# Attention over channels followed by a mixture of adapters: a planner with a finer model of the DMA rings, and the order of work that comes out of it

## The chip, the cores and the metric

The kernel runs on one core of a Trainium2 chip. Its time is the device time of one execution in microseconds (us), lower is better. A core has a matrix engine (TensorE, PE in the profile), two engines for elementwise work (VectorE, DVE; ScalarE, ACT), GpSimd (POOL) and SyncE (SP), which here issue transfers, and 16 DMA engines that all transfers share. A chunk below is 128 rows of 256 numbers, one row per SBUF partition.

## The reference

Four batches of q, k and v, each 6400 x 256 in float32. Columns of q and k are normalized over the 6400 rows; a 256 x 256 score matrix per batch goes through a softmax and multiplies v. Of the result x (25600 x 256) eight small adapters of rank 16 are gated, the two best of each row kept.

```python
qn = q / (norm(q, axis=1) + 1e-06);  kn = k / (norm(k, axis=1) + 1e-06)
a = softmax(kn.transpose(0, 2, 1) @ qn / tau)        # [4, 256, 256]
x = (v @ a).reshape(25600, 256)
logits = x @ w_gate                                  # 8 experts
topk = the two largest of each row;  w = softmax over these two
out = x + sum over the two of w * ((x @ A[e]) @ B[e])
```

## The kernel before, in words

**Tiles.** A batch is 50 chunks. q and k of a batch come in three pieces each of 17, 17 and 16 chunks (`QK`); v comes in five pieces of 10 chunks (`V`), and so does the output. The loads read float32 and write bfloat16 into SBUF, which is why GpSimd issues them (line 578, one instruction for a piece). Only the first four chunks of q and of k of batch 0 come as float32, by SyncE and ScalarE (line 574), into an output slot, and ScalarE casts them. The output is stored in float32 by SyncE (line 928): one store of 1,280 KB per piece, and for the last two pieces three stores each (512, 512, 256 KB; `FINE`).

**Work of a batch.** For each chunk, `G` adds k-transposed times q to two PSUM accumulators (line 593) and, unless the chunk's group is in the set `OFF`, the squares of k (line 597) and q (602), for the norms. For a group in `OFF` (a group is five or six chunks of either q or k) ScalarE squares it instead (line 615, step `sq`) and VectorE adds the groups up (line 621, `add`). After chunk 49 a short chain of small steps on all engines (`accs`, `n2`, `rsqrt`, `rq_ps`, `s`, `exp`, `aT`, `waA`, `a`) turns the accumulators into the softmax matrix and its product with the gate and the first adapter weights (`waA`).

For each piece of v: `T` transposes it on TensorE (line 788), `Te` brings it to SBUF (`vT`), then the gate logits and the first adapter product: a piece in the set `MERGED` makes both in one product (`ZL`, line 812) and copies them to SBUF (`ZLe`, four copies); another piece makes the logits alone (`log`, line 826), and later the adapter product (`Z`, line 879). Eight small VectorE steps and a tanh on ScalarE form the gate; `Ze` multiplies (line 890); `gzT` transposes the gated values (line 902); `Y` computes attention output plus the second adapter product into PSUM, two chunks at a time, five for a piece (lines 915 and 920); `Ye` copies them to an output slot on ScalarE or VectorE (lines 769 and 771); `store` sends the slot off.

**Order.** Nothing is ordered by hand except the loads. `make_plan` writes down every step with the engine or engines it may run on, the time it takes, a rank, and the buffers it takes and gives back (`STORE`: six PSUM banks, six q or k pieces, three v pieces, four transposed pieces, seven output slots, and so on). `Plan.run` then plays the program through once in Python, before anything runs: an engine that is free takes the ready step with the lowest rank, a load is issued when its buffer is free and fewer than eight are out, and two queues of transfers, loads and stores, share a bandwidth. The order in which steps were started is the order in which each engine's instructions are written; the chip then keeps that order engine by engine and waits on semaphores for the data. So the planner's numbers do not delay anything on the chip by themselves, they only choose the order.

The constants that steer it: `WORDS` is the order of the loads after the three pieces of batch 0's q and k (`q10` is piece 0 of batch 1's q and k together, `v23` piece 3 of batch 2's v). `AHEAD` and `SQ` move the ranks of transposes and squares forward, `SAFE` is a reserve that the planner adds to a load's landing, `HEAD` the time before the first transfer moves. `HOLD` names stores that wait until a given load has landed, so that they do not take DMA time from loads before that. It is done by a tiny transfer on SyncE's queue (step `hold`, line 645): it copies 16 numbers of the last chunk of that load to a scrap tile, so it waits for the load, and every store behind it on SyncE's queue waits too. `FIRST` and `PARTS` split the first and last q and k pieces. Every output slot and every v slot is a tile of its own, taken from the pool under a name with its number.

Of the kernel before, what the change touches and what calls it, by code (L numbers as in the profile page):

```python
# [18 lines left out]
class Step:  # L19
# [3 lines left out]
    def __init__(self, key, eng, deps, rank, take, give, size=0.0):  # L23
        self.packet = max(size, 0.08)
        self.key, self.eng, self.deps, self.rank = key, eng, deps, rank
        self.take, self.give, self.size = take, give, size
        self.users, self.place = [], {}
        self.ready, self.end, self.on = 0.0, None, None
        self.left = len(deps)
        self.only = next(iter(eng)) if len(eng) == 1 else None  # L30
# [38 lines left out]
class Plan:  # L69

    LAT = 0.07
    DMA_LAT = 1.8
    ENGINES = ("PE", "DVE", "ACT", "POOL", "SP")
    ISSUE = 0.55
    ISSUE_LAT = 1.8
    STORE_LAT = 1.4
    OUT = 8

# [15 lines left out]

    def run(self, head):
# [4 lines left out]
        loads, queue, stores = list(self.loads), [], []  # L100
        now, out, left = 0.0, 0, sum(s.key[0] != "warm" for s in self.steps.values())
        free["POOL"] = 0.2
        clock = Clock()

# [5 lines left out]
        def can_take(s):  # L110
            return all((kind, name) in held or self.store[kind] for kind, name in s.take)

        def start(s, eng):
            for kind, name in s.take:
                if (kind, name) not in held:
                    held[kind, name] = self.store[kind].pop(0)
                    s.place[kind] = held[kind, name]
            s.on = eng
            s.t = now
            self.out.append(s)  # L120

# [5 lines left out]
        while left:  # L127
            again = False
            if (loads and free["POOL"] <= now + 1e-9 and out < self.OUT and can_take(loads[0])):
                s = loads.pop(0)  # L130
                start(s, "POOL")
                out += 1
                free["POOL"] = now + self.ISSUE
                push(free["POOL"], "free", None)
                push(now + self.ISSUE_LAT, "asked", s)
                again = True
            for e in self.ENGINES:
# [3 lines left out]
                for s in wait[e]:  # L141
                    if not can_take(s) or (s.key[0] == "warm" and not clock.idle(now)):
                        continue
# [3 lines left out]
                    if best is None or (s.rank, s.seq) < (best.rank, best.seq):  # L147
                        best = s
# [9 lines left out]
                else:  # L158
                    push(free[e], "end", best)
# [3 lines left out]
            busy = [x for x in (queue, stores) if x]  # L163
            t = events[0][0] if events else float("inf")
            base = max(now, head)

            share = sum(x[0].packet for x in busy)
            if busy:
                t = min(t, base + min(x[0].size / x[0].packet for x in busy) * share)
            assert t < float("inf"), [s.key for s in self.steps.values() if s.end is None][:20]  # L170
            if t > base:
                for x in busy:
                    x[0].size -= (t - base) * x[0].packet / share
                    if x[0].size < 1e-6:
                        push(t + self.DMA_LAT, "landed", x[0])
                        out -= x is queue
                        x.pop(0)
            now = max(now, t)
            while events and events[0][0] <= now + 1e-9:
                _, _, what, s = heapq.heappop(events)  # L180
                if what == "asked":
                    queue.append(s)
                elif what == "store":
                    stores.append(s)
# [3 lines left out]
                elif what == "landed":  # L188
                    push(now + (SAFE if s.on == "POOL" else 0.0), "end", s)
                    for u in s.users:  # L190
                        if u.key[0] == "hold":
                            u.left -= 1
                            if u.left == 0:
                                push(now, "ready", u)
                elif what == "end":
# [6 lines left out]
                    for u in s.users:  # L202
                        u.left -= u.key[0] != "hold"
                        if u.left == 0 and u.eng and u.key[0] != "hold":
                            push(now + (0.0 if s.on == u.only else self.LAT), "ready", u)
# [10 lines left out]
V = ((0, 1), (1, 1), (2, 1), (3, 1), (4, 1))  # L216
# [13 lines left out]

def make_plan(B, order, ahead):
# [6 lines left out]
    for kind, b, i in order:  # L238
        if kind == "v":
            p.add(("load", "v", b, i, V[i][0] * PC, V[i][1] * PC), {}, (), 0, take=(("v", (b, i)),),  # L240
                  size=LOAD * V[i][1] * PC + 0.062)
            continue
        for c, n in PARTS.get((b, i), QK[i:i + 1]):
            for h in "qk":
                p.add(("load", h, b, i, c, n), {}, (), 0, take=(("qk", (h, b, i)),), size=LOAD * n + 0.062)

    for h in "qk":
        p.add(("cast", h), {"ACT": 0.6}, [("load", h, 0, 0) + PARTS[0, 0][0]], 0)
    p.loads[2].size += 0.5
    for b in range(B):  # L250

        for i, (c0, n) in enumerate(QK):
            for c in range(c0, c0 + n):
# [8 lines left out]
                p.add(("G", b, c), {"PE": 0.442 - 0.112 * sum((b, group_of(c), w) in OFF for w in "kq")}, deps,  # L262
# [4 lines left out]
        for w in "kq":  # L267
# [5 lines left out]
            for x, g in enumerate(halves):  # L273
                c, n = GROUPS[g]
                i = max(i for i, q in enumerate(QK) if q[0] <= c)
                p.add(("sq", w, b, g), {"ACT": 0.2 + 0.2125 * n},
                      [k for k in p.steps if k[:4] == ("load", w, b, i) and k[4] < c + n and c < k[4] + k[5]]
                      + [("cast", w)] * ((b, c) == (0, 0)), pos["qk", b, i] - SQ, take=(("ssq", (w, b)) if x == 0 else ("sq", (w, b, g)),),
                      give=(("qk", (w, b, i)),))
                if x:  # L280
                    p.add(("add", w, b, g), {"DVE": 0.15 + 0.268 * n},
# [4 lines left out]
            if halves:  # L286
                p.add(("red", w, b), {"DVE": 1.9}, [before], pos["qk", b, len(QK) - 1] - 1, give=(("ssq", (w, b)),))
                p.add(("n2p", w, b), {"PE": 0.35}, [("red", w, b), ("G", b, NC - 3)], -100, take=(("bank", ("n2p", w, b)),))
# [698 lines left out]
```

## Time and profile before

| | before |
|---|---|
| median of 3 runs (254.35 to 254.46) | 254.4 us |
| profiled execution, its own time | 254.46 us |
| its span | 252.7 us |
| mean granted TensorE clock | 0.986 |
| busy: TensorE, VectorE, ScalarE, GpSimd | 217.8, 192.7, 151.1, 27.1 us |
| HBM read and written | 78.91 MB and 26.21 MB, 416 GB/s over the span |
| loads issued by GpSimd (20 of v, 14 each of q and k), KB written each | 640; 512 to 1,088 |
| stores of the output | 18 of 1,280 KB, 4 of 512 KB, 2 of 256 KB |

The page of a profile shows the span in 40 slices of 6.3 us; each digit is the busy share of a slice in tenths, and a row of GB/s says what the DMA engines moved. A casting load counts there with the bytes it writes, half of those it reads. A second part lists the DMA queues: q0 is the queue of GpSimd's loads, q1 that of SyncE's stores. A third follows the work that ended last back through what released it. A table of stretches gives the busy time of every engine between two instants (the number of instructions in brackets), then the granted clock, the DMA share and GB/s; the DMA share can exceed 1, because packets of two queues overlap in the records.

### The profile page before, as it was taken

What the parts mean: (1) busy time and instruction counts of PE and PEld (TensorE: products, weight loads), DVE (VectorE), ACT (ScalarE), POOL (GpSimd) and SP (SyncE); (2) the same over time, 40 slices, a digit from 0 to 9 for tenths busy, and PEclk for the clock granted to TensorE, in tenths of its full rate; (3) what the DMA queues carried; (4) which work ended last, traced back from release to release, by engine and by line L of the source; (5) the groups of instructions that cost most, each with busy time, mean ns of one, the idle gap of its engine ahead of it and who ended that gap; (6) DMA issues with size and microseconds to landing.
All of it is one profiled execution on the core that took longest, in us unless ns stands there. A gap on an engine that the chain in (4) does not pass through costs nothing.

```text
span 252.7 us, 5852 instructions
## 1 busy us (share of the span) xinstructions
PE 217.8 (86%) x2357; PEld 193.0 (76%) x2357; DVE 192.7 (76%) x528; ACT 151.1 (60%) x269; POOL 27.1 (11%) x54
## 2 busy tenths in 40 slices
PE   0274995988999998689999999889999979999990
PEld 0162882876999996579899899779999769999980
DVE  0055589869899987588899899489898898889850
ACT  5454427546786543975667768362674846657671
POOL 7003010040002002000500100500000000000000
PEclk9998899999999999999999999999999999999997
DMA  8999999999999999999999999999999999999996
GB/s 251 217 217 209 211 223 208 217 218 215 215 217 241 303 305 298 224 213 221 210 215 220 215 217 217 211 212 313 317 251 353 322 341 317 337 392 415 404 408 249
DMA packets 11243, 66.70 MB, mean 264 GB/s; under 512 B 1360, under 2 KB 1744, under 8 KB 6608
## 3 DMA queue, kind: packets, MB, share of 16 engines
q0 software_dynamic: 6912, 38.80, 74.4%
q1 hardware_dynamic: 3968, 26.87, 26.1%
q10 hardware_dynamic: 336, 0.66, 0.8%
q8 instruction: 18, 0.29, 0.4%
q14 instruction: 9, 0.07, 0.1%
HBM read 78.91 MB, written 26.21 MB: 416 GB/s over the span
## 4 chain that ended last, share of the span: by engine, by line
PE 53%; DMA 32%; issue 5%; DVE 4%; ACT 2%; POOL 1%; POOLq 0%; DVEq 0%
DMA v<-in_v_dram 18%; PE Y_ps L915 13%; PE acc L593 10%; DMA qk<-in_q_dram 10%; PE Y_ps L920 6%; PE T_ps L788 5%; PE ZL_ps L812 5%; DMA qk<-in_k_dram 5%; PE gzT_ps L902 4%; PE acc L597 3%; PE acc L602 2%; PE Z_ps L879 1%; ACT a_exp L715 1%; DVE a_bf L763 1%; PE log_ps L826 1%
## 5 line engine op out<-in xcount | busy, mean ns | idle before, releaser
L593 PE MATMUL acc<-qk 128*128 128x256 bf16 x400 | 69.6, 282 | 17.0 <-DMA qk<-in_k_dram 9.4
L915 PE MATMUL Y_ps<-a_bf,vT 128*128 128x256 bf16 x400 | 60.0, 273 | 0.2 <-DVE acc_sb L710 0.2
L621 DVE TENSOR_TENSOR ssq<-ssq,sq 128x1280 f32<-128x1280 f32 (+1 forms) x27 | 43.4, 1606 | 19.6 <-ACT sq L615 19.6
L769 ACT COPY y<-Y_ps 128x512 f32<-128x512 f32 x79 | 46.2, 586 | 16.6 <-PE Y_ps L920 13.5
L593 PEld LDWEIGHTS <-qk 128*128 128x128 bf16 x400 | 34.2, 101 | 20.7 <-DMA qk<-in_k_dram 11.5
L615 ACT ACTIVATE sq<-qk 128x1280 f32<-128x1280 bf16 (+1 forms) x27 | 36.9, 1368 | 17.7 <-DVE ssq L621 16.6
L915 PEld LDWEIGHTS <-vT 128*128 128x128 bf16 x400 | 38.9, 98 | 4.7 <-issue 0.3
L920 PE MATMUL Y_ps<-ball,gzT 128*128 128x256 bf16 x200 | 38.2, 273 | 0.0
L597 PE MATMUL acc<-qk 128*128 128x128 bf16 x242 | 34.5, 224 | 0.0
L788 PE MATMUL T_ps<-ident,v 128*128 128x128 f32 x200 | 27.6, 274 | 0.6 <-DVE waA_sb L757 0.4
L769 ACT COPY vT<-T_ps 128x512 f32<-128x512 f32 (+1 forms) x44 | 21.2, 510 | 10.9 <-PE T_ps L788 10.5
L597 PEld LDWEIGHTS <-qk 128*128 128x128 bf16 x242 | 24.4, 101 | 3.5
L890 DVE TENSOR_TENSOR gz<-zl,gateg 128x256 bf16<-128x256 f32 x70 | 26.3, 445 | 0.3
L578 POOL DMA_DIRECT2D v<-in_v_dram x20 | 11.5, 576 | 133.7 <-PE T_ps L788 92.8
L788 PEld LDWEIGHTS T_ps<-ident,v 128*128 128x128 f32 x200 | 22.3, 141 | 1.6 <-DVE waA_sb L757 0.6
L602 PE MATMUL acc<-qk 128*128 128x128 bf16 x168 | 23.4, 222 | 0.0
L902 PE MATMUL gzT_ps<-ident,gz 128*128 128x128 f32 x100 | 20.9, 281 | 2.6 <-DVE gateg L868 1.4
L920 PEld LDWEIGHTS <-gzT 128*128 128x128 bf16 x200 | 19.6, 98 | 2.3
L812 PE MATMUL ZL_ps<-waA_sb,vT 128*128 128x136 bf16 x280 | 19.5, 223 | 1.7 <-DVE waA_sb L757 1.5
L771 DVE COPY gzT<-gzT_ps 128x256 f32<-128x256 f32 (+1 forms) x40 | 15.0, 380 | 7.1 <-PE gzT_ps L902 5.6
L812 PEld LDWEIGHTS <-vT 128*128 128x128 bf16 x280 | 17.7, 98 | 2.4 <-issue 2.1
L615 ACT ACTIVATE ssq<-qk 128x1536 f32<-128x1536 bf16 x8 | 11.9, 1489 | 11.4 <-DMA qk<-in_q_dram 7.4
(80 smaller groups left out, 271.3 us busy)
## 6 DMA issues: line engine op xcount, KB each, us to landing
out_dram<-y SPq DMA_DIRECT2D x18, 1280.0 KB, 16.7
v<-in_v_dram POOLq DMA_DIRECT2D x20, 640.0 KB, 20.5
qk<-in_q_dram POOLq DMA_DIRECT2D x7, 1088.0 KB, 23.7
qk<-in_k_dram POOLq DMA_DIRECT2D x7, 1088.0 KB, 28.4
qk<-in_q_dram POOLq DMA_DIRECT2D x4, 512.0 KB, 19.2
qk<-in_k_dram POOLq DMA_DIRECT2D x4, 512.0 KB, 22.5
qk<-in_q_dram POOLq DMA_DIRECT2D x2, 1024.0 KB, 19.4
qk<-in_k_dram POOLq DMA_DIRECT2D x2, 1024.0 KB, 23.8
```

The lines of the kernel that those rows point to most:

```text
L593: nc.tensor.matmul(acc[ic][:, 0:256], kt[:, j, ic::CC], qt[:, j, :], start=c == 0, stop=False, skip_group_check=True)
L597: nc.tensor.matmul(acc[ic][:, 256:384], kt[:, j, ic::CC], kt[:, j, ic::CC], start=False, stop=False, skip_group_check=True)
L602: nc.tensor.matmul(acc[ic][:, 384:512], qt[:, j, ic * P:(ic + 1) * P], qt[:, j, ic * P:(ic + 1) * P], start=False, stop=c == NC - 1, skip_ ...
L615: nc.scalar.activation(out[:, 0:n, :], t[:, j:j + n, :], ACT.Square)
L621: nc.vector.tensor_tensor(out=t, in0=t, in1=held["sq", (w, b, g), ""][:, 0:n, :], op=OP.add)
L769: nc.scalar.copy(out, in_)
L788: nc.tensor.matmul(ps[:, j, :], vt[:, c + j, :].bitcast(FP32), W["ident32"], is_transpose=True, start=(j == 0), stop=(j == n - 1))
L812: nc.tensor.matmul(ps[:, j, :], vT_of(b, i, c + j)[:, :, ic], st[b]["waA"][:, ic, :], start=(j == 0 and ic == 0), stop=(j == n - 1 and ic ...
L890: nc.vector.tensor_tensor(out=pairs[:, h].rearrange("p c (e r) -> p c e r", e=E), in0=z[:, 2 * h:2 * h + 2, :].rearrange("p c (e r) -> p c ...
L902: nc.tensor.matmul(ps[:, j, :], pairs[:, j * P:(j + 1) * P], W["ident32"], is_transpose=True, start=(j == 0), stop=(j == n // 2 - 1))
L915: nc.tensor.matmul(ps[:, j, :], vT_of(b, i, c + j)[:, :, ic], st[b]["a"][:, ic, :], start=(j == 0 and ic == 0), stop=False, skip_group_che ...
L920: nc.tensor.matmul(ps[:, j, :], pair[:, :, j], W["B"], start=False, stop=(j == 1), skip_group_check=True)
```

## The change

Four things are changed together.

- **The planner's model.** Where two queues shared a bandwidth, there are now two rings whose rows (eight for a transfer, one row per partition of a DMA engine, and a last entry for the semaphore) pass in turn through a short pipe; a landing gets a reserve that grows with time. The engines' step times are replaced by others, with a tail after which the result is seen (`TAIL`).
- **How a held store waits.** The step `hold` and its tiny transfers are gone. A store named in `HOLD` gets a semaphore dependency on the load itself. As all SyncE instructions, it is at the head of its queue while it waits.
- **Tiles.** All output slots are one tile `Y`, all v slots one tile `VS`; a slot is a part of it. (Options to load or store several pieces at once, `PAIRS` and `SPLIT`, are there but empty.)
- **Constants.** `WORDS`, `HOLD`, `PARTS`, `OFF`, `MERGED`, `AHEAD`, `SQ`, `SAFE` and `HEAD` get new values, and the order of all instructions follows. `OFF` has 42 groups (233 chunks) where it had 35 (195): by batch 56, 50, 71 and 56 chunks after 61, 49, 45 and 40. `MERGED` has 10 pieces where it had 14.

The diff, cut to its core:

```diff
 class Plan:
-    LAT = 0.07
-    DMA_LAT = 1.8
+    TAIL = {"PE": 0.164, "DVE": 0.083, "ACT": 0.1}
+    LAT = 0.037
...
+        def fill():
+            nonlocal turn, ahead
+            while ahead < self.PIPE and (rings[0] or rings[1]):
+                turn = 1 - turn if rings[1 - turn] else turn
+                s = rings[turn][0]
+                if s.rows:
+                    s.rows -= 1
+                    us, last = s.size * self.FETCH + self.ROW[turn], None
+                else:
+                    rings[turn].pop(0)
+                    us, last = self.SEM[turn], s
+                pipe.append((us, last))
+                ahead += us
...
+def held_by(p, b, i):
+    kind, d, j = HOLD[b, i]
+    return [k for k in p.steps if k[:4] == ("load", kind, d, load_of(d, j) if kind == "v" else j)][-1]
...
-WORDS = ('q10 v00 v01 v02 q11 v03 q12 v04 v10 v11 q20 v12 v13 v14 q21 v20 v21 v22 q22 q30 '
-         'q31 q32 v23 v24 v30 v31 v32 v33 v34')
-HEAD = 2.6
+WORDS = ('v00 q10 q11 v01 q12 v02 v03 q20 v04 q21 v10 q22 v11 q30 v12 q31 v13 v14 v20 v21 q32 v22 v23 v24 v30 '
+         'v31 v32 v33 v34')
+HEAD = 5.05
...
-AHEAD = 2.7
-HOLD = {(0, 0): ('k', 3, 1), (0, 1): ('k', 1, 2), (0, 4): ('k', 3, 2), (1, 0): ('k', 3, 1),
-        (1, 1): ('k', 3, 2), (1, 2): ('k', 3, 2), (1, 3): ('k', 3, 2), (1, 4): ('k', 3, 2),
-        (2, 0): ('k', 3, 1), (2, 1): ('k', 3, 2), (2, 4): ('k', 3, 1)}
-PARTS = {(0, 0): ((0, 2), (2, 15)), (0, 2): ((34, 8), (42, 8)), (3, 2): ((34, 8), (42, 8))}
+AHEAD = 4.1
+HOLD = {(0, 0): ('v', 3, 3), (0, 1): ('v', 3, 2), (0, 2): ('v', 1, 1), (0, 3): ('v', 3, 4), (0, 4): ('v', 3,
+        0), (1, 1): ('v', 3, 4), (1, 2): ('v', 2, 2), (1, 3): ('v', 1, 4), (2, 0): ('v', 2, 3), (2, 1):
+        ('k', 3, 1), (2, 2): ('v', 3, 4), (2, 4): ('k', 2, 1), (3, 0): ('v', 0, 0), (3, 1): ('v', 2, 1), (3,
+        4): ('v', 2, 1)}
+PARTS = {(0, 0): ((0, 4), (4, 13)), (0, 2): ((34, 8), (42, 8)), (3, 2): ((34, 8), (42, 8))}
...
-SQ = 2
-SAFE = 0.5
-MERGED = {(0, 1), (0, 2), (0, 3), (1, 0), (1, 1), (1, 2), (1, 3), (1, 4), (2, 0), (2, 1), (2, 2),
-        (2, 4), (3, 2), (3, 4)}
+SQ = 4.5
+SAFE = 0.9
+MERGED = {(0, 0), (1, 2), (1, 4), (2, 1), (2, 2), (2, 3), (2, 4), (3, 0), (3, 1), (3, 2)}
...
+    Y = sbuf.tile([P, STORE["y"] * PC, C], FP32, name="y")
+    VS = sbuf.tile([P, STORE["v"] * PC, C], BF16, name="v")
...
-    def do_hold(s, kind, b, i):
-        if kind == "k":
-            src = held["qk", ("k", b, i), ""][0:1, QK[i][1] - 1, 0:16]
-        else:
-            src = held["v", (b, i), ""][0:1, V[i][1] * PC - 1, 0:16]
-        nc.sync.dma_start(scrap, src)
...
     def do_store(s, b, i, c, n):
         lo = i * PC + c
-        nc.sync.dma_start(out_v[b, :, lo:lo + n, :], held["y", (b, i), ""][:, c:c + n, :])
+        at_y = at["y", (b, i)] * PC + c
+        p = 0
+        for rows in SHARES if (b, i) in SPLIT else (P,):
+            r = nc.sync.dma_start(out_v[b, p:p + rows, lo:lo + n, :], Y[p:p + rows, at_y:at_y + n, :])
+            if (b, i) in HOLD and not p:
+                tc.add_manual_dep(r.ins, loaded[held_by(plan, b, i)],
+                                  mybir.DependencyInfo(mybir.DependencyClass.Sync, mybir.DependencyReason.DATA),
+                                  reason="held")
+            p += rows
```

## The prediction

> **What bounds the kernel now.** I read the page from its second part downwards: the forty slices first, then the DMA queues, then the chain of waits, and last the stretches that these pointed to.
>
> ```profile
> PE   0274995988999998689999999889999979999990
> DVE  0055589869899987588899899489898898889850
> DMA  8999999999999999999999999999999999999996
> GB/s 251 217 217 209 211 223 208 217 218 215 215 217 241 303 305 298 224 213 221 210 215 220 215 217 217 211 212 313 317 251 353 322 341 317 337 392 415 404 408 249
> ```
>
> The DMA row has a 9 in every slice but the first and the last; no engine has that. A load reads float32 and writes bfloat16, and the GB/s row counts the smaller side: 217 there is 434 GB/s read. The queues give the two kinds of work:
>
> ```profile
> q0 software_dynamic: 6912, 38.80, 74.4%
> q1 hardware_dynamic: 3968, 26.87, 26.1%
> ```
>
> q0 holds the casting loads (38.80 MB written, 77.6 read), q1 SyncE's stores and first load. So first of all I price the DMA engines by stretch. In the stretch table the last column is GB/s, the one before it the DMA share; PE's busy time stands third.
>
> ```profile
> 100.00:160.00 60.00, 56.52 (x604) 51.02 (x602) 49.84 (x120) 41.93 (x74) 4.77 (x9) 1.00 1.04 218
> 168.00:200.00 32.00, 31.03 (x368) 28.96 (x367) 28.27 (x86) 18.72 (x38) 0.67 (x2) 1.00 1.05 302
> 225.00:235.00 10.00, 10.00 (x129) 9.47 (x127) 8.95 (x29) 6.83 (x17) 0.00 (x0) 1.00 1.02 429
> 235.00:246.00 11.00, 11.00 (x112) 9.93 (x110) 7.53 (x24) 7.89 (x16) 0.00 (x0) 1.00 0.96 400
> 246.00:253.00 7.00, 0.77 (x8) 0.44 (x5) 0.00 (x0) 1.25 (x3) 0.00 (x0) 0.73 0.61 243
> ```
>
> Loads alone (100 to 160 us; 0.32 MB of a store at its start taken out) read about 431 GB/s. Stores alone (225 to 235) move 429. Where both run, the queue view gives for 170 to 225 us:
>
> ```profile
> q1 hardware_dynamic: 1365, 11.94, 52.9%
> q0 software_dynamic: 1298, 5.61, 50.0%
> ```
>
> that is (2 x 5.61 + 11.94) / 55 us = 421 GB/s; 80 to 100 us gives (2 x 2.41 + 3.61) / 20 = 421 as well. The floor, if nothing were lost: 77.6 MB / 431 = 180.0 us, 26.87 / 429 = 62.6, the other queues' 1.0 MB 2.4, together 245.0 us. About 1.7 us are lost before the first bytes flow (0 to 1 us 4 GB/s, 1 to 2 us 127), and about 1.0 us lies behind the last byte. That makes 247.7 where the span is 252.7: **5.0 us are lost**, and no change of order can win more. Where they go:
> - 75 us of mixed loads and stores at 421 instead of 430: 75 x 9/430 = 1.6 us.
> - The end. From 235 us on 6.1 MB move in 17.7 us; at 429 they would take 14.2, and about 0.8 us follow the last landing: 2.7 us lost. Stores run short: their work is not yet computed.
> - The rest, 0.7 us, is spread.
>
> Why stores run short is seen in the chain of waits. From 207 us it is TensorE with hardly another name on it, to the end of the last product:
>
> ```profile
> 244.81 0.44 PE Y_ps L915 x4
> 245.46 0.44 PE Y_ps L915 x4
> 246.11 0.44 PE Y_ps L915 x4
> 246.55 0.23 PE Y_ps L920 x2
> 246.81 0.59 ACT y L769
> ```
>
> So two things end together: the DMA engines' bytes, and TensorE's backlog, whose last piece is stored only from 247.4 us on; that store lands 4.5 us after its issue. To finish earlier, both must give.
>
> **The change, part by part.** Sums are against the profiled execution: span 252.7, its own time 254.46, so 1.76 us lie around the span; the median of the runs shown, 254.4, is the same within 0.06.
>
> *Squares (OFF).* 35 groups with 195 chunks of 128 rows become 42 with 233: +38 chunks. Each takes two 128-column products off TensorE. Four 256-column products take 0.44 us in the chain, so two of 128 take 0.11: 38 x 0.11 = **-4.2 us of TensorE**. ScalarE gets seven more squares: the 1,280- and 1,536-wide rows, 1,275 and 1,485 ns, differ by 0.21 us a chunk and leave 0.22 fixed: 38 x 0.21 + 7 x 0.22 = +9.5 us. VectorE gets seven more additions, by 1,487 and 1,754 ns 0.27 a chunk and 0.15 fixed: +11.3 us. They lie beside DMA time as long as VectorE has room.
>
> *Merged pieces: 14 become 10.* A merged piece costs TensorE one chain entry of 1.18 us (ZL), the other form 0.48 (log) and 1.12 (Z): 4 x 0.42 = **+1.7 us of TensorE**. ScalarE and VectorE drop four evacuations for each piece (two of about 0.5, two of 0.4 us) and gain one of 0.24: 4 x (1.8 - 0.24) = -6.2 us. TensorE's net is -2.5 us.
>
> *Stores wait on loads themselves.* Three one-line copies to the scrap tile go, 0.51 to 0.60 us each on SyncE's queue; the queue was idle for over 70 us before the first, so nothing is late next: 0. What they did, a store waiting for a load, is added at 15 stores (12 without the three of batch 3, whose loads land long before them). Behind a waiting store stand all later stores on SyncE's queue, and the output slot of each. Before, the queue opened at 183 us for ten stores at once. After, six slots (pieces 00, 01, 03, 04, 11, 22) are held for loads of batch 3's v. Hence fewer stores beside loads: some nine instead of thirteen, and four more as filling for the end. Removing 4 of 13 from the mixed stretches is worth 4/13 of 1.6 = **-0.5 us**; the bounds are 0 (the stores fall in a mixed stretch anyway) and -1.6 (no mixing at all).
>
> *Order of loads.* v00 goes ahead of q10 and k10; the q and k of batches 2 and 3 come one or two places earlier; behind the last q and k stand eight v loads instead of seven. A v load is 1.31 MB read, 3.04 us at 431. GpSimd issues each in 0.53 to 0.58 us, and rings were deep (16 to 29 us from issue to landing in the middle), so moving an issue past others costs nothing by itself: all 46 stay. The earlier q and k bring the last softmax chain, in which TensorE stood idle 2.2 us (7.81 busy in the ten us from 200), forward to a time when DMA has other work, and every deferred store lets the last load land some 3 us sooner (now it is issued at 213.7 and lands 10.9 us later).
>
> *At the end* TensorE thus has 2.5 us less to do and at best 2.2 us less to wait: up to 4.7 us, of which only what DMA can follow counts. Of DMA's 2.7 us lost there, the last store's 4.5 us and the stores of 512 and 256 KB stay as they are; I take half, **-1.3 us**; bounds 0 and -2.7, the row between them being 235 to 246 us with 400 of 429 GB/s, a fault of 7% that more stores in the queue would mend.
>
> *Code of the planner, tiles.* One tile for all output slots and one for all v slots, instead of single ones, keeps the same bytes; waits it might add or drop are not in this trace: bounded by one store's issue, 0.33 us, on either side; taken as 0. The new first-part split loads the same four chunks as before: 0.
>
> [...] In 80 to 100 us the two queues moved 417 packets each, strictly one for one. [...]
>
> **Sum:** -0.5 - 1.3 = -1.8 us: span 250.9, **time 252.6**; by both outer bounds 250.1 to 254.4.
>
> **Rivals.**
> 1. *DMA nearly full to the end.* All of the end and most of the mixing are won: -4.3 at most, by the rows above about -3.5: 251.0, reaching from 249.8 to 251.6. For it: six held stores are 18 us of filling (3.06 us each). Against it: small last stores.
> 2. *Nothing won.* The tail stays TensorE's: eight v pieces behind the last q and k instead of seven. One piece is T 1.09, ZL 1.18, gzT 0.55, Y 5 x 0.655: 6.1 us against 4.7 at best won. 254.4, from 253.8 to 255.0. That the change does not do what it says ends here too: loads and stores that miss the planned instants give the old mixture.
> 3. *Slower: output slots.* Seven slots, six of them held. A store among loads landed 10.8 us after issue or later; with 3.3 us for its five products and half a microsecond around, a slot turns once in 14.6 us. With two slots free that is 7.3 a piece, 1.1 over what TensorE needs; for three pieces, +3.3: 257.7. It decides once fewer than three slots turn while v20 to v30 are loaded. Against it: up to 167 us all seven were held before too, and TensorE had other work.
> 4. *Slower: VectorE.* Batches 2 and 3 get 42 of the added chunks (26 and 16), 42 x 0.27 + 9 x 0.15 = 12.7 us more VectorE between 100 and 200 us, where it is busy 84 of 100. It can hand evacuations to ScalarE (65 of 100 there), which itself gets 10.8. If it hands over only half of the surplus and its idle share must stay, (84 + 6.3)/0.84 - 100 = 7.5 us, less the 4.7 that TensorE gains: +2.8, 257.2. It decides over about 95% busy.
>
> **How the numbers follow.** Forecast (251.6 to 253.8) 0.45; rival 1 0.14; rival 2 0.13; rival 3 0.16 and rival 4 0.12, both 255 to 260. A difference within 0.2% (253.9 to 254.9) can hardly be told from none by a measurement of this kernel. Faster: 0.45 + 0.14 and a sliver of rival 2, 0.60; same 0.12; slower 0.28. The range leaves out rival 1 below 250.0 (0.03) and about half of rivals 3 and 4, above 257.0 (0.13): 250.0 to 257.0. The forecast's own is 251.6 to 253.8.
>
> **What would show it.** Right: DMA share 1.0 from 235 to 247 us with over 415 GB/s, the last load landed before 222 us, TensorE finished before 245, loads unmixed for longer. Wrong: a 7 or 8 in DMA's slices before the last (rival 3 or 4), TensorE idle for an output copy between 160 and 215 us (rival 3), VectorE at 95% in 100 to 200 us with TensorE waiting for it (rival 4), or a chain that again is TensorE alone to 246 us (rival 2).

## The result and the profile after

The changed kernel takes 262.4 us (median of 4 runs, 261.7 to 263.0) where the kernel before takes 254.4: 1.031 times as long, 95% interval 1.029 to 1.034. The profiled execution took 262.58 us, its span is 260.8 us and the granted clock 0.931. The prediction, 252.6 us with a range to 257.0, had the wrong sign.

Three rows of the page (the granted TensorE clock in tenths, the DMA share, GB/s), 40 slices, now of 6.5 us each, and two of its queues:

```profile
PEclk9959986689999999999995999999988999999995
DMA  8999999999999999999999988999995999999995
GB/s 253 214 215 213 213 222 215 215 210 220 211 217 218 219 215 209 220 214 261 267 295 236 211 180 143 213 215 233 372 368 144 360 256 216 420 423 427 433 410 234
...
q0 software_dynamic: 6912, 38.80, 73.4%
q1 hardware_dynamic: 3872, 26.87, 25.0%
```

The bytes are those of before. What is new stands in the DMA row: two 8s, at 150 to 163 us, and a 5, at 196 to 202. GB/s falls to 143 and 144 there. The clock row has a 5 ahead of the first place (137 to 143 us) and two 8s at the second (189 to 202 us). Stretches show it closer (PE's busy time third, then PEld, DVE, ACT, POOL; granted clock, DMA share and GB/s at the end):

```profile
135.00:140.00 5.00, 3.92 (x21) 3.58 (x22) 3.70 (x23) 3.68 (x6) 0.25 (x1) 0.59 1.04 276
155.00:160.00 5.00, 5.00 (x68) 4.80 (x66) 4.54 (x7) 4.39 (x10) 2.91 (x6) 1.00 0.56 88
190.00:195.00 5.00, 2.91 (x28) 2.48 (x26) 2.57 (x16) 2.34 (x7) 0.00 (x0) 0.89 1.00 388
195.00:200.00 5.00, 5.00 (x35) 4.31 (x34) 3.21 (x18) 3.98 (x10) 0.53 (x1) 0.77 0.44 173
225.00:250.00 25.00, 25.00 (x288) 22.97 (x286) 15.88 (x61) 20.13 (x45) 0.00 (x0) 1.00 1.01 424
```

For about four microseconds each time the DMA engines have almost nothing to do, while TensorE is busy. A ledger makes microseconds of it: for each stretch, (twice the bytes of q0, plus those of the other queues) / 430 GB/s (an estimate, from the 431 that loads alone read and the 429 that stores alone moved) is the time that the bytes need; what is left of the stretch is lost.

| us lost in stretch | 141–154 | 154–160 | 160–178 | 178–195 | 195–202 | 202–225 | 225–250 |
|---|---|---|---|---|---|---|---|
| before | 0.0 | 0.0 | 0.4 | 0.2 | 0.1 | 0.5 | 1.2 |
| after | 0.3 | 3.2 | 0.3 | 0.8 | 3.6 | 1.7 | 0.4 |

The difference is 10.2 - 2.4 = 7.8 us; the spans differ by 8.1. Both kernels move the same bytes, so over the whole span the ledger must differ by what the spans differ; it cannot say why, but it says where: 6.7 of the 7.8 us stand in two stretches of 6 and 7 us in which the DMA rings (the queues of transfers that are handed over but not done) run empty.

**Why they run empty.** The DMA view of both stretches (forty slices of each stretch; queue, packets, MB, share; a transfer, KB, us from issue to landing), first 154 to 160 us:

```profile
DMA  8986858648432150300000000199906063899699
...
q0 software_dynamic: 129, 0.58, 59.2%
```

then 195 to 202 us:

```profile
DMA  9594959898502121200000000000993314794989
...
q0 software_dynamic: 58, 0.30, 30.8%
q1 hardware_dynamic: 101, 0.85, 29.0%
...
v<-in_v_dram POOLq DMA_DIRECT2D x1, 640.0 KB, 6.6
```

In the first stretch there is no store at all (SyncE issues none between 129 and 177 us, while four finished pieces of batch 0 are held); in the second the store in flight ends and no other follows. Loads come from GpSimd, whose timeline shows each v load with the wait before it:

```profile
156.77 0.53 POOL L629 DMA_DIRECT2D v<-in_v_dram  x1 [16.50 <-PE T_ps L830]
...
198.76 0.53 POOL L629 DMA_DIRECT2D v<-in_v_dram  x1 [15.76 <-PE gzT_ps L944]
```

A v load needs one of three slots, and a slot comes free when TensorE has transposed the piece in it. v21 goes out at 156.77, when the loads ahead of it have already landed; v31 at 198.76. Behind v21 stand five more loads in GpSimd's order; they follow one after another as soon as it is out, from 157.62 to 159.69 us. Before, v31, v32, v33 and v34 were issued at 191.55, 199.87, 204.97 and 213.66 us, the first two 7 and 6 us earlier than after, the last two 2 us earlier and at the same time. There too no load was issued for 27 us ahead of v31, and it cost nothing: SyncE had issued six stores between 183.8 and 186.2 us and a seventh at 190.8 us, which landed 35.7 us later. The queues from 195 to 202 us, before:

```profile
q1 hardware_dynamic: 179, 1.62, 56.4%
q0 software_dynamic: 149, 0.67, 46.7%
```

After, such stores are put off, and while a load is late there is nothing else to move.

**Why the loads are late.** Of the second place the chain of waits tells it (start, us, what):

```profile
177.97 14.19 DMA out_dram<-y
192.23 1.08 ACT y L812 x2
...
194.74 1.71 PE T_ps L830 x8
```

ScalarE's copy to an output slot waits 3.0 us for a store to free the slot; TensorE waits for ScalarE, and the transposes that free the v slot come after it. The first place begins at 134 us, in TensorE's timeline:

```profile
135.22 0.58 PE L687 MATMUL n2p_ps<-ones,ssqq 128*128 128x1 f32 x4 [0.53 <-DVE ssqq L681]
136.66 1.94 PE L830 MATMUL T_ps<-ident,v 128*128 128x128 f32 x8 [0.86 <-DMA v<-in_v_dram]
```

TensorE has small gaps (2.33 us busy of 132.5 to 135.9), the granted clock is 0.50 from 135.9 to 142.7 us, and eight transposes take 1.94 us where the kernel before took 1.04 for eight, at a clock of 1.00 (at 197.77 us).

A half clock did not cost DMA time everywhere. In the changed kernel it came three times before 54 us as well, each time for 6.8 us, and the ledger loses nothing there (0.2 us or less, either way, at 13 to 20, 36 to 44 and 47 to 54 us); the first of them:

```profile
13.00:19.80 6.80, 5.96 (x33) 4.31 (x34) 1.60 (x1) 2.25 (x2) 0.00 (x0) 0.50 1.05 220
```

Both kernels already contain filler products (512 columns of zeros) where the planner's own model of the clock sees TensorE idle: 39 before, the last at 207.8 us; 24 after, and none behind 61.2 us:

```profile
L820 PE MATMUL warm_ps<-zeros,ident x24: 377/391/634, 7.8 to 61.2; 128*128 128x512 bf16 x24
```

So the new plan has none at either place, and the clock fell there: at the first after 2.33 us busy between 132.5 and 135.9, at the second after 1.91 us busy between 190 and 194.

### The profile page after: what moved, and what is told of

Read it like the earlier page. It is cut to its first block, busy times and chain, and to the rows that moved or that the text cites. A ratio compares the mean times of both kernels' runs of the same rounds, so it can differ in the third digit from the quotient of the medians.

```text
span 260.8 us, 5792 instructions
## 1 busy us (share of the span) xinstructions
PE 223.8 (86%) x2346; PEld 196.9 (75%) x2346; DVE 182.1 (70%) x498; ACT 167.6 (64%) x301; POOL 26.2 (10%) x54
## 4 chain that ended last, share of the span: by engine, by line
PE 47%; DMA 29%; DVE 16%; ACT 3%; issue 1%; SPq 0%; DVEq 0%; ACTq 0%; POOLq 0%
DMA v<-in_v_dram 20%; PE Y_ps L957 12%; PE T_ps L830 8%; DVE ssq L672 6%; PE Y_ps L962 6%; DMA out_dram<-y 5%; PE acc L644 5%; PE ZL_ps L854 4%; PE gzT_ps L944 3%; DMA qk<-in_q_dram 3%; PE Z_ps L921 2%; DVE a_bf L806 1%; PE acc L653 1%; DVE y L814 1%; PE acc L648 1%
## 5 line engine op out<-in xcount | busy, mean ns | idle before, releaser
L644 PE MATMUL acc<-qk 128*128 128x256 bf16 x400 | 76.7, 291 | 13.1 <-DMA qk<-in_k_dram 6.9
L672 DVE TENSOR_TENSOR ssq<-ssq,sq 128x1280 f32<-128x1280 f32 (+1 forms) x34 | 54.5, 1604 | 23.9 <-ACT sq L666 23.9
L666 ACT ACTIVATE sq<-qk 128x1280 f32<-128x1280 bf16 (+1 forms) x34 | 46.5, 1367 | 27.6 <-DVE ssq L672 20.5
L957 PEld LDWEIGHTS <-vT 128*128 128x128 bf16 x400 | 38.3, 99 | 4.2
L653 PE MATMUL acc<-qk 128*128 128x128 bf16 x200 | 28.6, 226 | 0.0
L932 DVE TENSOR_TENSOR gz<-Z_ps,gateg 128x256 bf16<-128x256 f32 x50 | 19.5, 442 | 5.4 <-PE Z_ps L921 5.1
L812 ACT COPY gzT<-gzT_ps 128x256 f32<-128x256 f32 (+1 forms) x44 | 14.2, 345 | 9.2 <-PE gzT_ps L944 8.8
L648 PE MATMUL acc<-qk 128*128 128x128 bf16 x134 | 19.5, 228 | 0.0
L629 POOL DMA_DIRECT2D v<-in_v_dram x20 | 10.7, 541 | 85.6 <-PE T_ps L830 56.0
L932 DVE TENSOR_TENSOR gz<-zl,gateg 128x256 bf16<-128x256 f32 x50 | 19.1, 444 | 0.1
L629 POOL DMA_DIRECT2D qk<-in_q_dram x14 | 7.6, 546 | 102.0 <-PE acc L653 24.1
L944 PEld LDWEIGHTS gzT_ps<-ident,gz 128*128 128x128 f32 x100 | 12.1, 142 | 7.3 <-ACT y L812 2.3
```

Source lines behind the costliest of these rows:

```text
L629: loaded[s.key] = nc.gpsimd.dma_start(t[:, 0:n, :], src[b, :, c:c + n, :]).ins.name
L644: nc.tensor.matmul(acc[ic][:, 0:256], kt[:, j, ic::CC], qt[:, j, :], start=c == 0, stop=False, skip_group_check=True)
L648: nc.tensor.matmul(acc[ic][:, 256:384], kt[:, j, ic::CC], kt[:, j, ic::CC], start=False, stop=False, skip_group_check=True)
L653: nc.tensor.matmul(acc[ic][:, 384:512], qt[:, j, ic * P:(ic + 1) * P], qt[:, j, ic * P:(ic + 1) * P], start=False, stop=c == NC - 1, skip_ ...
L666: nc.scalar.activation(out[:, 0:n, :], t[:, j:j + n, :], ACT.Square)
L672: nc.vector.tensor_tensor(out=t, in0=t, in1=held["sq", (w, b, g), ""][:, 0:n, :], op=OP.add)
```

## The experiments

The letters are those of the expectations. Theory A: the new order has no reserve, v slots and output slots are handed on just in time, and a late TensorE leaves the load ring empty. B: the new mechanism (single tiles, stores that wait on loads) costs the time. C: too many output slots are held for the last loads. D, a sharper form of A: the loads come no later than where it does no harm; what the new order lacks is stores that are waiting in their ring when a load is late. Two more rivals have no letter: the granted clock alone, and VectorE.

**The mechanism alone.** The order of before, with single tiles for output and v slots, and stores waiting on the loads themselves:

```diff
-        nc.sync.dma_start(scrap, src)
...
+        if (b, i) in HOLD:
+            tc.add_manual_dep(r.ins, loaded[HOLD[b, i]], ...)
```

> The order of before, kept instruction by instruction, with the two mechanical parts of the change alone: all output slots in one tile and all v slots in one, and held stores that wait on the load's own semaphore in place of the tiny copies. Theory A (the new order has no reserve: v slots and output slots are handed on just in time, and a late TensorE leaves the load ring empty): the mechanism costs nothing, 254.4, within 0.5. Theory B (the single tiles or the new waits hold up more than they should): over 256. Theory C (too many output slots are held for the last loads): as A, 254.4.

254.62 us (10 runs) against 254.49; ratio 1.0008, interval 0.9998 to 1.0019. B falls: mechanism and tiles cost at most 0.5 us by the interval, and nothing that can be told from zero; the 8 us are in the order.

**Order kept, waits left out.** The stores keep their places and wait for no load:

```diff
-            if (b, i) in HOLD and not p:
+            if False:
```

> The changed kernel with its order kept, without the stores' waits on loads: a store still stands at its place in SyncE's queue, but waits only for its own data. Theory A: the stores' places, not the waits, set when slots come free, and the empty load ring near 155 us is not touched: 262, from 261 to 263. Theory B: the waits were the cost, 259 or less. Theory C: the two stores held until v22 has landed leave a little sooner, 260 to 262.

259.70 us, one run. Timed again:

> The changed kernel without the stores' waits on loads, timed in rounds, as its single look of 259.7 was under every theory's 261 but B's. If the waits cost something in their place: 259 to 260.5 in all runs. If the look was only spared a half clock by chance (it had 1.0 at 136 to 143 us): runs spread from 259.5 to 263.

260.44 us (259.69 to 262.08), ratio 1.024, interval 1.020 to 1.029. That is some 2 us of the 8; it lies below A's 261 to 263 and within C's 260 to 262. Part of it may be the clock's: on the pages of both profiled runs the clock row has a 9 (0.9 or more) in the slices from 130 to 141 us, where the changed kernel's clock is 0.74 from 134 to 138 and 0.50 from 138 to 142 us, and the one run of 262.08 us is as slow as the changed kernel. Either way the waits as such are not the cause; 6 us stay without them.

**The clock.** Three 512-column products ahead of `n2p` and four ahead of the transposes of piece (1,2), with zeros, into banks that the step overwrites:

```diff
+        for _ in range(WARM_N.get((w, b), 0)):
+            nc.tensor.matmul(ps, W["ident"], W["zeros"][:, None, :].to_broadcast([P, 2, 256]), start=True, stop=True)
```

> The changed kernel with seven filler products of 512 columns more, three ahead of batch 2's last norm sum and four ahead of the first transpose of piece 12, in the gap of TensorE at 134.6 to 136.7 us after which its granted clock was 0.5 for 6.7 us. Theory A: the clock stays at 1.0, TensorE gains about 3.3 us by 155 us, the load of v21 is issued about 3 us sooner, the load ring is empty for some 1.5 us instead of 4.5, and the time is 258 to 260. Theories B and C: the clock is better but the time stays over 261.

259.68 us, one run; and timed:

> The changed kernel with the seven filler products, timed in rounds. Theory A, a half clock that costs 2 to 3 us when it comes: 259.0 to 260.5 in all runs, with a spread under that of the changed kernel (261.7 to 263.0).

260.27 us, ratio 1.023, interval 1.022 to 1.025. In the timed kernel all runs but one (260.66) lie in the expected range, and they spread by 0.5 us instead of 1.3. The clock stays 1.00 at the place:

```profile
138.00:142.00 4.00, 3.98 (x44) 3.42 (x42) 2.32 (x9) 3.47 (x8) 0.53 (x1) 1.00 1.03 225
```

So the fillers win 2.1 of the 8 us in the changed kernel. That is the half clock at 136 us with what follows from it: the one at 194 us is gone too, though a copy still waits up to 3.4 us for a store there. The clock alone is not the whole story: 5.8 us remain.

**The output slot.** The store of piece (0,4) goes behind that of (1,0) and waits for nothing; seven later pieces take slots that are then free:

```diff
+    steps.insert(1 + next(n for n, s in enumerate(steps) if s.key[:3] == ("store", 1, 0)), early_store)
+    for x, n in (((1, 4), 4), ((2, 0), 5), ((2, 1), 2), ((2, 2), 4), ((2, 3), 5), ((2, 4), 2), ((3, 1), 5)):
+        at["y", x] = n
```

> The changed kernel with one output slot more in turn: the store of piece 04 stands behind that of piece 10 on SyncE's queue and waits for no load, and pieces 14 to 24 and 31 take their slots accordingly; all other instructions keep their order. Theory C: no copy of Y waits for a store at 185 to 192 us, TensorE's gap of 2 us and the half clock behind it go, the load ring does not run empty at 197 us: 256.5 to 259. Theory A alone: the empty ring near 155 us stays, or comes some 3 us later because a store is mixed in; with only the second one gone 258 to 260. Theory B: 261 or more.

258.81 us, one run, and no copy waits for a store any more. C and A alone had both left room for this time; but the first empty stretch, which A had expected to stay, shrank too, to 0.3 us, with a store now in the ring from 128 us on. With the filler products too:

> The changed kernel with both: one output slot more in turn (the store of piece 04 behind that of piece 10) and the seven filler products in TensorE's gap at 135 us. The issues of the v loads stand against the planner's own times as follows so far: changed kernel +3.0 us at v21, +3.3 at v30, +7.3 at v31, +6.9 at v34; filler alone +1.2, +1.5, +4.4, +4.1; slot alone +2.6, +3.1, +2.7, +2.5. If the two delays are separate and add up, here about +1.2 throughout and a time of 256.5 to 257.5, some 5.3 us less than the changed kernel. If the second delay is only the first one's consequence, the slot adds nothing to the filler: 259.7. What stays over the kernel before, 2 to 3 us, would be the order's own.

258.50 us, ratio 1.016, interval 1.014 to 1.017. This lies between the two forecasts, 256.5 to 257.5 and 259.7: slot and clock neither add up nor are one. Together they account for half of the 8 us. Compute is then free of both: the last output copy starts at 245.53 us, 1.3 us earlier than in the kernel before (246.81). Yet 4 us stay.

**VectorE.** e9_slot_warm without the eleven additions of batch 2's squares:

> The same, with VectorE's eleven additions of batch 2's squares left out (so that batch's norms lack them; the squares are still taken). VectorE is busy all the time from 120 to 137 us in the changed kernel. If VectorE holds TensorE up there (the prediction's rival 4), another 1.5 to 3 us go: 254 to 255.5. If not, within 0.7 of the kernel with the additions.

258.19 us, one run. Between 100 and 160 us VectorE is busy 41.3 instead of 55.6 us, and the time moves by 0.3. VectorE does not hold the kernel up there.

**Reserve, four stores.** (0,4) and (0,1) wait for v14, (0,0) and (0,3) for v24, and go ahead of the stores of batches 1 and 2 that follow:

```diff
+MOVED = [((0, 4), (1, 0)), ((0, 1), (0, 4)), ((0, 0), (1, 4)), ((0, 3), (0, 0))]
...
+WAIT = {(0, 4): ('v', 1, 4), (0, 1): ('v', 1, 4), (0, 0): ('v', 2, 4), (0, 3): ('v', 2, 4)}
```

> The changed kernel with a reserve of stores at the two places where its rings run empty: the stores of pieces 04 and 01 stand behind that of piece 10 and wait for the load of v14 (lands near 154 us), those of 00 and 03 behind piece 14's and wait for v24's (near 184 us); later pieces take the slots that come free sooner; all compute instructions keep their order. Theory D (the loads come no later than in a kernel where it does no harm; what the new order lacks is stores that are waiting in their ring when a load is late): DMA moves over 400 GB/s between 154 and 202 us, some 5 us of the loss go, 255 to 257. Theory C (slots alone): as with one slot more, 258.8. If the loads' lateness by shared rings costs TensorE as much as it fills: 258 to 261.

257.46 us, one run, 0.5 above D's range and 1.3 below C's. With fillers:

> The same with the seven filler products ahead of batch 2's norm sum and piece 12's first transpose. Theory D: with the rings full a TensorE that is a microsecond or two late at 155 us costs nothing, so within 0.7 of the kernel without the filler. Theory A: another 1 to 3 us less.

257.15 us, one run: within the 0.7 of D, not the 1 to 3 us of A, and without the fillers the clock was at 0.57 on average from 138 to 142 us. So with stores in the rings that half clock cost next to nothing, as far as one run each can tell. In the ledger of the run without fillers 154 to 160 us loses 0.4 and 195 to 202 loses 0.1, but 225 to 240 now loses 2.0 (1.2 with fillers): the stores that bridge the middle are missing at the end.

**Reserve, one store and two.** First e9_slot_warm with its early store waiting for v14:

> As the kernel with slot and filler, but the store of piece 04 waits until the load of v14 has landed (near 154 us), so that it takes no DMA time from the loads before. If that store's share of the rings was what made v21 late: v21 issued at +1.2 us against the planner's time (155.0), and 256.3 to 257.4. If the delays are one and the same: 258 to 259, with v21 at +2.5 again.

258.43 us, a miss. v21 is issued at 154.6 us instead of 156.2, but 1.4 us are lost at 195 to 202 and as much again up to 225 us. A load that is issued 1.6 us earlier was worth 0.1 us here. Then the store of (0,1) in addition, waiting for v24:

```diff
-MOVED = [((0, 4), (1, 0))]
-WAIT = {(0, 4): ('v', 1, 4)}
+MOVED = [((0, 4), (1, 0)), ((0, 1), (1, 2))]
+WAIT = {(0, 4): ('v', 1, 4), (0, 1): ('v', 2, 4)}
```

> The same, and the store of piece 01 stands behind piece 12's and waits for v24 (near 182 us) in place of v32. If what is left is lost in the rings' second gap (178 to 202 us, 2.8 us in the kernel with slot and filler): another 1 to 2 us less, 255 to 256. If the order of the compute instructions sets the end: within 0.7 of the run before.

255.44 us, ratio 1.004, interval 1.003 to 1.006. This pair is the plainest test of reserve, A's first half and D's whole. The nine v loads from 154 us on are issued at the same instants in both, to within 0.1 us (154.6, 182.4, 194.2, 201.7 and 209.2 among them), and the last output copy starts at the same time, first e13_slot_late, then e14_two_stores:

```profile
245.70 0.59 ACT y L826
```

```profile
245.75 0.59 ACT y L826
```

So compute is as late in the one as in the other; one store in the ring takes 3.0 us off. 195 to 202 us in e13_slot_late:

```profile
DMA  2099760999789989894995927899999989599899
```

and in e14_two_stores:

```profile
DMA  9898989869898999899898999999989879999999
...
q1 hardware_dynamic: 202, 1.82, 62.1%
q0 software_dynamic: 124, 0.60, 41.7%
...
v<-in_v_dram POOLq DMA_DIRECT2D x1, 640.0 KB, 10.6
```

No slice is empty. v32, issued at 201.65 us, takes 10.6 us to land where it took 9.0 in e13_slot_late; for the two v loads ahead of it, issued at 182.4 and 194.2 us, the median is 11.5 instead of 8.6. Sharing was slower for the loads and better for the kernel (255.44 against 258.43 us).

**Is the clock a cause by itself?** e14_two_stores without the filler products:

> The two moved stores of e14_two_stores, without its seven filler products, so that the granted clock is whatever the changed order makes it. Theory A (rings that run empty are the cause, the clock only one of the things that delay a load): with stores in the ring a delay of the clock costs at most the time by which TensorE ends later, below 1 us: 255.4 to 256.5. Rival (the clock by itself holds the kernel, the stores only helped where it was full): the half clock comes back at 136 us and costs the 2 to 3 us it cost in the changed kernel: 257.5 to 258.5.

256.74 us (255.9 to 257.5), ratio 1.008, interval 1.005 to 1.011, which just overlaps that of e14_two_stores. It lies between the two theories: a half clock is back, and costs about 1.3 us.

```profile
134.00:138.00 4.00, 1.33 (x10) 0.75 (x9) 3.65 (x23) 2.40 (x5) 0.00 (x0) 0.99 1.03 304
138.00:142.00 4.00, 4.00 (x27) 3.67 (x28) 0.81 (x3) 2.24 (x5) 0.54 (x1) 0.58 1.07 228
```

By these means it lasted some 3.4 us, half as long as in the changed kernel (0.74 and 0.50 in the same stretches, some 6.8 us). So these two stores do not hide a half clock, though theory A had wanted that. Of the 1.7 us between the two profiled runs the ledger from 141 to 250 us shows 0.5; the last output copy starts 0.9 us later (246.68 against 245.75).

**A third store.** e14_two_stores with the store of (0,0) as well, ahead of that of (1,2), waiting for v23:

```diff
+MOVED = [((0, 4), (1, 0)), ((0, 0), ('load', 'v', 2, 3)), ((0, 1), (1, 2))]
...
```

> e14_two_stores, and the store of piece 00 behind the issue of v23's load, waiting for v23 instead of v33, so that the store ring holds something from about 177 us on. In e14_two_stores the DMA engines lose 1.0 us at 178 to 195 us, nearly all at 179 to 183, where the loads end and the next stores have only just been issued. Theory A: 0.5 to 0.8 us of it are won, unless TensorE, now without idle time from 190 us to its last product at 246.3, holds the end: 254.6 to 255.1. Rival (the end is TensorE's): no change, 255.3 to 255.6. Slower than 255.8 if the earlier store delays v24 and through it the transposes.

257.92 us (255.8 to 259.4, ratio 1.010, interval 1.006 to 1.015), slower, but not for the reason given there. The waits, and the chain:

```profile
ACT y L827 <- DMA out_dram<-y: 2.9, 1, 2.9
```

```profile
180.85 10.99 DMA out_dram<-y
...
191.91 0.59 ACT y L827
```

The third store stands ahead of the one that frees the slot for the next piece. The wait for the output slot is back, v31 is issued at 198.23 instead of 194.24, and the DMA row has a new hole, a 7 and an 8 at 219 to 232 us:

```profile
DMA  8999999999999999999999999999999999789996
```

By the medians the slot costs 2.5 us here, but the four runs spread by 3.6 us and the profiled one is the slowest of them, so the size is rough. It is a control that was not meant as one. With the store of (0,4) also waiting for v13 instead of v14:

> e16_third_store, and the store of piece 04 waits for v13 (landed about 149.5 us) instead of v14, so that it is in the ring before the loads end at 154 us. Theory A: the 1.0 us that the DMA engines lose at 154 to 160 us falls to about 0.3, so up to 0.7 us less than e16_third_store: 254.0 to 254.8, near the kernel before. Rival (a store among the last loads delays v20, and so the v loads behind it, as the store issued at 130 us did): 0.5 to 1.5 us more than e16_third_store.

257.15 us (256.3 to 257.8): the slot wait (4.3 us) hides the effect, but 154 to 160 us loses 0.1 instead of 0.8. So that edit was tried alone, on e14_two_stores:

> e14_two_stores with the store of piece 04 waiting for v13 instead of v14, and no third store. In e17_earlier that wait brought the loss of the DMA engines at 154 to 160 us from 0.8 to 0.1 us, with v21 issued at 154.93, no later than before. Theory A: 0.5 to 0.9 us less than e14_two_stores, 254.5 to 255.0, no more than the kernel before by 0.2%. Rival (TensorE holds the end, which has no idle time from 190 to 246 us there): as e14_two_stores, 255.2 to 255.7.

255.04 us (11 runs) against 254.47; ratio 1.0023, interval 1.0014 to 1.0032; between A's 255.0 and the rival's 255.2. By the ledger 154 to 160 loses 0.1 instead of 1.0, 178 to 195 0.2 instead of 1.0, while 195 to 202 and 225 to 250, together, lose 1.2 more. TensorE is busy 55 of the 56 us from 190 to 246, but it is not what holds the end. Its last output copy starts 1.8 us earlier than in the kernel before (246.81), and the span is still 253.2 against 252.7 us:

```profile
244.98 0.58 ACT y L826
```

Against the kernel before, the largest difference in the ledger is at 195 to 202 us (0.6 instead of 0.1). No version tried beats the kernel before.

**Planner and constants apart.** The new planner with the old `WORDS`, `AHEAD`, `HOLD`, `OFF`, `SQ` and `MERGED`:

> The new planner with the old load order, held stores, squares, merged pieces and the two rank offsets: a third order, searched for by nobody. If the planner's model is what makes the order bad: over 262. If the constants do: near 254 to 256. If constants and planner only fit each other (an order is the result of a replay in which every constant was chosen): over 257, and so for the converse run.

267.58 us. The old planner with the new ones:

> The old planner with the new load order, held stores, squares, merged pieces and rank offsets. If the constants make the order bad: 261 or more. If the planner's model does: near 254 to 256. If they only fit each other: over 257.

265.14 us. Both are slower than the change as a whole (one run each): alone the halves cost 13.1 and 10.7 us, together 8. That fits the third forecast, that constants and planner only fit each other, though each half also meets the forecast by which it is bad by itself; no half of the change is the good one. Why each loses was not followed further. More v slots or output slots, the direct cure for late loads, were not tried.

## Why the prediction was wrong, step by step

- **The step that failed** is in "Order of loads": rings were deep (16 to 29 us from issue to landing), so "moving an issue past others costs nothing by itself". That was the depth of most earlier loads of the old order. The v loads at stake, v31 to v34, took 12.3, 11.5, 12.6 and 10.9 us even there, and what kept the DMA engines busy beside them was a ring of stores: six issued within 2.4 us, not ten at once. In the new order a v load is issued into an empty ring twice (5.9 and 6.6 us to landing), and the two stretches lose 6.8 us. The same putting-off of stores that was priced as filling for the end (-1.3) is what emptied the middle, by their places on SyncE's queue more than by their waits (e11_no_hold_timed); bytes moved to the end are missing before it. One store put back was worth 3.0 us (e14_two_stores).
- **The end, -1.3.** 225 to 250 us lost 0.4 instead of 1.2, but that is no longer the end: the span is 8 us longer. In the last 17.7 us of each span 3.5 us are lost before and 3.2 after, so 0.3 us of it came; in e18_two_earlier it is 3.5 again. The sign "over 415 GB/s from 235 to 247 us" appeared (428) while the forecast failed: with everything 8 us late these instants had a backlog of stores.
- **Mixing, -0.5.** The loads did run alone from about 141 to 178 us, and the ledger of 160 to 178 moved by 0.1 us.
- **Rival 3, output slots, +3.3.** The right kind of wait, at the place named (TensorE idle for an output copy between 160 and 215 us), and a price of the right size for another reason: it was not a matter of three pieces at 1.1 us but mainly of one wait of 3.0 us. Freeing the slot gained 3.6 us without fillers (e4_slot, one run) and 1.8 with them (e9_slot_warm), and putting the wait back cost roughly 2.5 (e16_third_store). The rest of the 8 us lies outside what the rival named.
- **The granted clock** had no term at all; 2.1 us by the fillers. Its mean, 0.986 before and 0.931 after, does not show that price: more than half of the added half-clock time lies before 54 us (clock 0.97 before and 0.81 after from 0 to 54 us), where the DMA engines lost nothing by it (0.2 us or less).
- **Rival 4, VectorE.** Not borne out: busy 86.7 of 100 us between 100 and 200, below the 95% from which it was to decide, and e10_no_adds took its added work away for 0.3 us.
- **Right:** mechanism and tiles at 0 (e1_mechanism). TensorE's saving: the trace has 334 products of 128 columns for the squares instead of 410, 200 of `ZL` instead of 280, and 80 more each of `Z` and `log`, at the sum's prices 2.5 us less; it was worth nothing. The sign named for rivals 3 and 4, "a 7 or 8 in DMA's slices before the last", appeared.
- **Small slips:** GpSimd's issues are 48 (20 + 14 + 14), not 46; the added groups of batches 2 and 3 are 8, not 9; 7.3 less 6.1 is 1.2 a piece. Nothing hangs on them.

How the 8 us divide follows from the order in which they were mended, and the parts are not independent: clock 2.1, then slot 1.8, then the two stores kept for the rings 3.1, then the earlier wait of (0,4) 0.4; 0.6 us over the kernel before stay. They are not TensorE's end, which is 1.8 us earlier than before; their cause stays open.

## What to carry to other kernels

The 9 in every slice of the DMA row before showed that the rings were not empty, not how much was in them (v34 landed 10.9 us after its issue, a store issued at 190.8 us 35.7 us after): before a transfer is moved or held, ask for each load that waits for a buffer what the other ring holds at that moment, and count the microseconds of it. Stores held back are filling for one place only; where loads are handed on just in time, one spare store in the ring can be worth more than an earlier load (here 3.0 us against 0.1). Before a store is placed ahead of others, look which buffer the ones behind it give back.

## What the runs showed of the hardware

The granted clock fell without a long pause of TensorE: in the two stretches ahead of the falls the longest was 2.04 us. In the changed kernel TensorE was busy 2.33 us between 132.5 and 135.9, and the clock was 0.50 from 135.9 to 142.7 us (0.94 on average from 135 to 136, which puts the fall at 135.9). With the fillers (e3_warm) it was busy 1.00, 1.00, 0.38 and 0.47 of the four microseconds from 134 to 138, and the clock stayed 1.00. From 190 to 194 us of the changed kernel it was busy 1.91 us, with a single wait of 2.04, and the clock was 0.50 from 193.9 to 197.3. These falls lasted 6.8 and 3.4 us and nearly doubled the transposes (1.94 and 1.91 us for eight, against 1.04 at a clock of 1.00), at the very place where they free a buffer. What sets the moment of a fall and its length was not shown.

Stores that were held back did not fill the rings. In the changed kernel SyncE issued no store between 129 and 177 us, while four finished pieces of batch 0 were held in output slots; between 156 and 159 us the DMA row has eleven slices of 0.15 us with 0 GB/s, eight of them in a row, from 156.55 to 157.75 us.
